# Unused bytes in the on-chip memory of an attention-and-two-MLPs kernel, so that the MLPs' operands begin at multiples of 512 bytes

## The chip, the core and the metric

The kernel runs on one core of a Trainium2 chip. The metric is the device time of one execution, in microseconds (us). Of three runs of the kernel before, the median is 1062.01 us (1061.28 to 1065.92).

On the core, TensorE (PE) multiplies: a LDWEIGHTS puts a stationary block of 128 x 128 into the array, a MATMUL streams a moving operand past it, up to 512 columns wide, and the result goes to PSUM. VectorE (DVE), ScalarE (ACT) and GpSimd (POOL) do the rest; SyncE (SP) issues most of the DMAs. Both operands of a product lie in SBUF, a memory of 128 partitions. A tile takes the same byte range of every partition, so one number, its start address within a partition, says where it lies.

## The reference

```python
def _attn_ref(q, k, v, s):                 # 4 batches, 8 heads, 576 positions, head size 64
    scores = scale * np.matmul(q, k.transpose(0, 1, 3, 2))
    cum = np.cumsum(np.maximum(s, 0.0), axis=-1)
    bias = -(cum[:, :, :, None] - cum[:, :, None, :])
    scores = np.where(causal, -1000000000.0, scores + np.minimum(bias, 0.0))
    attn = softmax(scores)
    return np.matmul(attn, v)

x = attention output as 2304 x 512
x = (relu(x @ w1_in) ** 2) @ w1_out        # 512 -> 2048 -> 512
h = x @ w2_in
return np.maximum(0.01 * h, h) @ w2_out    # 512 -> 2048 -> 512
```

All of it is float32.

## The kernel before

**Products.** Every MLP operand is split into a high and a low part in the type float32r, and a product is made of three passes (high by high, high by low, low by high: `PASSES`, L67). A weight tile is `[128, 2, 512]`: 2048 bytes of high part and 2048 bytes of low part. A stationary block is 128 columns of it, 512 bytes, so the four blocks of one part begin 512 bytes apart. A moving operand is a row of 512 columns (2048 bytes), or of 256 columns in the last of the five blocks of tokens (`BLOCKS`, L68).

**Stages.** Attention runs over 16 pairs of heads in a pipeline that is written out by hand (`attention`, L484). Its queue of matmuls is filled up with the first product of the first MLP (`up1`, L456; matmuls at L476, tile `xs` moving against `w` stationary), whose results go to DRAM as `gscr`. After the last pair the rest of that product runs. Then `down1` (L645; matmuls at L656) multiplies `gh`, which is `gscr` read back and split, moving, by the weights `wo` of `w1_out`, stationary. Then `layer2` (L666) does both products of the second MLP: at L691 `xs` moves against `w`, at L681 the activations `g` are stationary and the weights of `w2_out` move: 14 of its 16 slices lie in tiles `wo`, two in tiles `wx` (`EX = 2`, L61).

**Where the tiles lie.** The tiles are laid out in pools, one behind the other from the low end, in the order in which the pools are opened and the tiles are first asked for. First come the constants (pool `c`: `ident`, `mask`, `mask4`), then the 16 tiles `w0` to `w15` (`wpool`), then the pools of the stages. Attention's pool `at` lies above those of `up1`. The pools `s2` (staging of weights) and `w2` (the tiles `wo0` to `wo15`) are laid from the upper end downwards (`side="right"`). A tile begins at a multiple of 32 bytes. Since the constants have lengths that are no multiple of 512, and every tile of the MLPs is 2048 or 4096 bytes long, all tiles from one end share one remainder modulo 512.

In attention, each slot makes one tile `t` of scores and one small tile `m` of row minima (`maxima`, L303, `TB = 3` buffers of each), and each pair has one tile of row sums, `sums` (L329).

Of the kernel before, what the change touches and what calls it, by code (L numbers as in the profile page):

```python
# [7 lines left out]
F32 = mybir.dt.float32  # L8
# [14 lines left out]
def attention_then_two_mlps(  # L23
# [28 lines left out]
    P = 128  # L52
# [10 lines left out]
    TB, VB, YB = 3, 4, 2  # L63
# [7 lines left out]
    cpool = ctx.enter_context(tc.tile_pool(name="c", bufs=1))  # L71
# [9 lines left out]
    ident = cpool.tile([P, P], F32, name="ident")  # L81
    mask = cpool.tile([P, S], BF16, name="mask")
    mask4 = cpool.tile([P, S // 2], BF16, name="mask4")
    win, wout = {}, {}

    def bank(tag):
# [91 lines left out]
    def running_sums(at):  # L178

        sp, cum = [at.tile([BH, S], F32, tag="t", name="t", bufs=TB) for _ in range(2)]  # L180
        one, neg = [at.tile([BH, S], F32, tag="yt", name="yt", bufs=2) for _ in range(2)]
        ka = at.tile([BH, 2, S], F32R, tag="pT1", name="ka", bufs=2)
        nc.sync.dma_start(sp, s.rearrange("b h t -> (b h) t"))
        nc.gpsimd.memset(one, 1.0)
        nc.gpsimd.memset(neg, -1.0)
        yield
        nc.vector.tensor_scalar(sp, sp, 0.0, 1.0 / QK_SCALE, ALU.max, ALU.mult)
        nc.vector.tensor_tensor_scan(cum, one, sp, 0.0, ALU.mult, ALU.add)
        nc.vector.tensor_copy(ka[:, 0], cum)
        nc.vector.tensor_tensor(ka[:, 1], cum, f32(ka[:, 0]), ALU.subtract)  # L190
        nc.sync.dma_start(aug[:, 0:2, 0], one.unsqueeze(1).to_broadcast([BH, 2, S]))
        nc.sync.dma_start(aug[:, 2:4, 1], neg.unsqueeze(1).to_broadcast([BH, 2, S]))
        nc.sync.dma_start(aug[:, 0:2, 1], f32(ka))
        nc.scalar.dma_start(aug[:, 2:4, 0], f32(ka))
# [14 lines left out]
    def load_qk(at, x, i=None):  # L209

        b, g = pairs[x].b, pairs[x].g
        if not i:
            raw["q"] = at.tile([P, 2, S], F32, tag="qr", name="qr")
            raw["k"] = at.tile([P, 2, S], F32, tag="kr", name="kr")
        for src, dst, queue in ((k, raw["k"], nc.scalar if i == 0 else nc.sync), (q, raw["q"], nc.sync)):
            for e in range(2):
                for db in range(2):
                    p0 = 64 * e + 32 * db
                    dd = slice(db * 32, (db + 1) * 32)
                    if i is None:  # L220
                        nc.sync.dma_start(
                            dst[p0:p0 + 32].rearrange("p h (a d) -> p (h a) d", d=32),
                            src[b, 4 * g + 2 * e:4 * g + 2 * e + 2, :, dd].rearrange("h (a t) d -> t (h a) d", t=32))
                    else:
                        issued = queue.dma_start(
                            dst[p0:p0 + 32, i].rearrange("p (a d) -> p a d", d=32),
                            src[b, 4 * g + 2 * e + i, :, dd].rearrange("(a t) d -> t a d", t=32))
                        if queue is nc.scalar:
                            raw["issued"] = issued.ins
# [73 lines left out]
    def maxima(at, x, kind, e):  # L303

        p = pairs[x]
        t = at.tile([P, S], F32, tag="t", name="t", bufs=TB)  # L310
        m = at.tile([P, 2], F32, tag="m", name="m", bufs=TB)

        def reduce(sc, msk, a, z, first, m):
            return nc.vector.tensor_tensor_reduce(t[:, a:z], sc, msk, -QK_SCALE, first, ALU.add, ALU.min, m).ins  # L314

        sc = p.sc[e]
        if kind == 0:
            tiles = ((0, P, 0), (P, 3 * P, 1))
            for a, z, c in tiles:
                done = reduce(sc[:, a:z], mask[:, S - z + a:], a, z, 3.0e38, m[:, c:c + 1])  # L320
        elif kind == 4:
            tiles = ((0, S, 0),)
            reduce(sc[:, :S // 2], mask[:, :S // 2], 0, S // 2, 3.0e38, m[:, 1:2])
            done = reduce(p.sc[1][:, :S // 2], mask4, S // 2, S, m[:, 1:2], m[:, 0:1])
        else:
            tiles = ((0, (kind + 1) * P, 0),)
            done = reduce(sc[:, :(kind + 1) * P], mask[:, S - (kind + 1) * P:], 0, (kind + 1) * P, 3.0e38, m[:, 0:1])
        if kind == 0 and e == 0:
            p.sums = at.tile([P, 10], F32, tag="sums", name="sums", bufs=3)  # L329
        T = {0: 0, 2: 2, 3: 3, 4: 4}[kind]  # L330
        p.t = t
        return t, m, tiles, p.sums, 2 * T + e, done
# [111 lines left out]
    def up1_x(mp, j, c, bufs):  # L444

        n, w = BLOCKS[j]
        xf = mp.tile([P, W], F32, tag="xf", name="xh", bufs=2)
        nc.sync.dma_start(xf[:, :w], xscr[c, :, n:n + w])
        yield
        t = mp.tile([P, 2, W], F32R, tag="xs", name="xs", bufs=bufs)  # L450
        xs[j, c] = t
        split([t[:, z, :w] for z in range(2)], xf[:, :w])
# [3 lines left out]
    def up1(mp, j, tick=None):  # L456

        n, w = BLOCKS[j]

        def close(fc, h, gs):  # L460
            r = mp.tile([P, W], F32, tag="r", name="r", bufs=2)
            nc.scalar.activation(r[:, :w], h[:, :w], AF.Relu)
            done = nc.scalar.activation(gs[:, fc % 2, :w], r[:, :w], AF.Square)
            if fc % 2:
                nc.scalar.dma_start(gscr[fc - 1:fc + 1, :, n:n + w].rearrange("f p t -> p f t"), gs[:, :, :w])
            if tick is not None:
                tick(done.ins)

        todo = None
        for fc in range(FC):  # L470
            if fc % 2 == 0:
                gs = mp.tile([P, 2, W], F32, tag="gs", name="gs", bufs=GB1)
            h = bank("h")
            for c in range(KC):
                for y, (a, z) in enumerate(PASSES):
                    nc.tensor.matmul(h[:, :w], win[0, fc][:, a, c * P:(c + 1) * P], xs[j, c][:, z, :w],  # L476
                                     start=(c == 0 and y == 0), stop=(c == KC - 1 and y == 2))
                if c == 0 and todo is not None:
                    close(*todo)
                yield  # L480
            todo = (fc, h, gs)
        close(*todo)

    def attention(at, mg, mx):  # L484
# [14 lines left out]
        sums = running_sums(at)  # L499
        next(sums)  # L500
        load_qk(at, 0, 0)
        warm = at.tile([P, 1], F32, tag="warm", name="warm")
        nc.vector.memset(warm, 0.0)
        with after(raw["issued"]):
            nc.scalar.activation(warm, warm, AF.Exp)
# [75 lines left out]
        for y in range(end + 13):  # L581
# [11 lines left out]
            if y < end:  # L593
                args = maxima(at, x, *STEPS[st])
                live[y] = args[0]
                behind = [args[-1], exponentials(*args[:-1])]
# [114 lines left out]
    with tc.tile_pool(name="mg", bufs=1) as mg, tc.tile_pool(name="mx", bufs=1) as mx:  # L711
        with tc.tile_pool(name="at", bufs=1) as at:
            attention(at, mg, mx)
        s2, w2 = [late.enter_context(tc.tile_pool(name=x, bufs=1, side="right", reuse_waits="tile"))
                  for x in ("s2", "w2")]
        weights = Conversions(s2)
        weights.add(2, [(1, 0, fc, f"o{fc}", w2) for fc in range(FC)])
        with tc.tile_pool(name="mt", bufs=1) as mt:
            for c in range(KC):
                for _ in up1_x(mt, B, c, KC):  # L720
                    pass
            for j in (B - 1, B):
                for _ in up1(mg, j, weights.tick):
                    pass
# [42 lines left out]
```

## Time and profile before

| | |
|---|---|
| median of three runs | 1062.01 us (1061.28 to 1065.92) |
| the profiled execution: time, span | 1064.36 us, 1062.6 us |
| PE busy | 1017.2 us (96%), 5312 matmuls |
| PEld (weight loads) busy | 837.3 us (79%) |
| DVE, ACT, POOL busy | 562.6, 520.2, 225.0 us |
| mean granted TensorE clock | 0.988 |
| attention with L476 beside it | 0 to about 394 us |
| rest of L476, then L656 | about 394 to 658 us |
| L691 and L681 | 658 us to the end |

The span is the time from the first to the last instruction; the time of the profiled execution holds 1.8 us more around it. [...]

### The profile page before, as it was taken

Reading aid. Unit: us, or ns where it says so; the run is one execution under the profiler, and the core shown is the slowest. Engines: PE = TensorE matmul, PEld = TensorE weight load, DVE = VectorE, ACT = ScalarE, POOL = GpSimd, SP = SyncE. Lnnn points to the kernel's source line nnn. Section 1 sums busy time; section 2 is a strip of 40 time slices with the busy share of each in tenths; the row PEclk is TensorE's granted clock in tenths of the full one; section 3 lists DMA queues with packets and bytes.
Section 4 is the critical chain, followed back from the end, with each engine's and each line's share of the span. In section 5 each row is a group of like instructions: output and inputs, shape, how many; then the busy total and the mean of one; then the engine's idle time right before and its main releaser. Section 6 shows DMA issues by size and latency. Waiting matters only on the chain.

```text
span 1062.6 us, 15075 instructions
## 1 busy us (share of the span) xinstructions
PE 1017.2 (96%) x5312; PEld 837.3 (79%) x5312; DVE 562.6 (53%) x1262; ACT 520.2 (49%) x1126; POOL 225.0 (21%) x294
## 2 busy tenths in 40 slices
PE   5878988899999999999999999999999999999998
PEld 3656777778888878888888889888888888888897
DVE  5767868874576524787865438753222322232322
ACT  3656867876687656763443334533312322322232
POOL 6445555652232002223211003210000000000000
PEclk9988999899999999999999999999999999999999
DMA  8737384674352244866765447411100200100010
GB/s 135 102 90 151 103 168 127 135 138 123 84 109 85 81 170 168 270 191 203 237 212 167 139 117 237 129 34 30 49 1 1 80 1 1 60 1 1 1 40 21
DMA packets 152476, 111.30 MB, mean 105 GB/s; under 512 B 98992, under 2 KB 121008, under 8 KB 152400
## 3 DMA queue, kind: packets, MB, share of 16 engines
q1 hardware_dynamic: 139072, 91.01, 33.0%
q10 hardware_dynamic: 13328, 19.32, 5.3%
q8 instruction: 42, 0.69, 0.3%
q14 instruction: 34, 0.28, 0.1%
HBM read 76.69 MB, written 33.62 MB: 104 GB/s over the span
## 4 chain that ended last, share of the span: by engine, by line
PE 60%; DMA 2%; DVE 1%; ACT 0%; issue 0%; ACTq 0%; SPq 0%; DVEq 0%
PE tr L681 19%; PE h L691 9%; PE S L691 9%; PE tr L656 8%; PE h L476 6%; PE h L656 4%; PE S L656 4%; DMA wst<-in_moe_w_out_dram 1%; DMA xh<-xscr 1%; DMA gl<-gscr 0%; DMA xscr<-xo 0%; ACT xs L440 0%; DVE wo L110 0%; DVE gh L441 0%; DVE wt L108 0%
## 5 line engine op out<-in xcount | busy, mean ns | idle before, releaser
L476 PE MATMUL h<-xs,w 128*128 128x512 f32 (+1 forms) x960 | 227.6, 381 | 2.2 <-DVE w L110 0.8
L476 PEld LDWEIGHTS h<-xs,w 128*128 128x128 f32 x960 | 162.1, 190 | 33.1 <-DVE xs L441 2.2
L681 PE MATMUL tr<-wo,g 128*128 128x512 f32 x756 | 186.0, 396 | 0.0
L681 PEld LDWEIGHTS tr<-wo,g 128*128 128x128 f32 x756 | 141.5, 188 | 32.6
L107 POOL TENSOR_TENSOR wt<-wt,wst 128x512 uint32<-128x512 uint32 x64 | 88.5, 1382 | 297.2 <-DVE wt L104 238.8
L697 DVE TENSOR_TENSOR r<-S,r 128x512 f32<-128x512 f32 (+1 forms) x40 | 25.5, 639 | 173.9 <-ACT r L696 173.9
L656 PE MATMUL tr<-gh,wo 128*128 128x512 f32 (+1 forms) x576 | 114.2, 358 | 0.0
L691 PE MATMUL S<-xs,w 128*128 128x512 f32 (+1 forms) x480 | 107.2, 369 | 1.0 <-ACT xs L440 1.0
L656 PEld LDWEIGHTS tr<-gh,wo 128*128 128x128 f32 x576 | 94.7, 188 | 16.9
L691 PE MATMUL h<-xs,w 128*128 128x512 f32 (+1 forms) x480 | 107.6, 369 | 0.0
L338 ACT ACTIVATE t<-t,m 128x128 f32<-128x128 f32 (+2 forms) x144 | 83.3, 580 | 36.1 <-DVE m L314 35.6
L691 PEld LDWEIGHTS S<-xs,w 128*128 128x128 f32 x480 | 84.8, 188 | 17.4 <-ACT xs L440 1.5
L691 PEld LDWEIGHTS h<-xs,w 128*128 128x128 f32 x480 | 85.0, 188 | 16.3
L696 ACT ACTIVATE r<-S 128x512 f32<-128x512 f32 (+1 forms) x40 | 22.2, 555 | 150.6 <-PE S L691 150.6
L441 DVE TENSOR_TENSOR gh<-gl,gh 128x512 fp32r<-128x512 f32 (+1 forms) x80 | 64.5, 809 | 52.8 <-ACT gh L440 52.6
L314 DVE CUSTOM_DVE_ANT_0 t<-S,mask 128x128 f32<-128x128 f32 (+2 forms) x144 | 64.8, 481 | 45.7 <-PE S L298 22.5
L440 ACT ACTIVATE gh<-gl 128x512 fp32r<-128x512 f32 (+1 forms) x80 | 46.3, 586 | 79.2 <-PE h L656 36.5
L348 PE MATMUL tr<-ident,t 128*128 128x128 f32 x384 | 70.5, 295 | 14.3 <-ACT t L338 12.9
L441 DVE TENSOR_TENSOR g<-r,g 128x512 fp32r<-128x512 f32 (+1 forms) x80 | 51.0, 644 | 38.5 <-ACT g L440 37.0
L348 PEld LDWEIGHTS tr<-ident,t 128*128 128x128 f32 x384 | 47.1, 148 | 30.2 <-ACT t L338 17.6
L102 ACT ACTIVATE wt<-wst 128x512 f32<-128x512 f32 x64 | 42.5, 664 | 57.7 <-DMA wst<-in_moe_w_in_dram 41.6
L440 ACT ACTIVATE g<-r 128x512 fp32r<-128x512 f32 (+1 forms) x80 | 46.7, 589 | 43.5 <-DVE r L697 43.5
(105 smaller groups left out, 1462.4 us busy)
## 6 DMA issues: line engine op xcount, KB each, us to landing
wst<-in_moe_w_in_dram SPq DMA_DIRECT2D x32, 512.0 KB, 4.0
gscr<-gs ACTq DMA_DIRECT2D x32, 512.0 KB, 4.4
wst<-in_moe_w_out_dram SPq DMA_DIRECT2D x32, 512.0 KB, 4.5
gl<-gscr SPq DMA_DIRECT2D x64, 256.0 KB, 3.0
xscr<-xo SPq DMA_DIRECT2D x32, 144.0 KB, 2.5
out_dram<-o SPq DMA_DIRECT2D x18, 256.0 KB, 2.4
xh<-xscr SPq DMA_DIRECT2D x16, 256.0 KB, 2.7
zscr<-ys SPq DMA_DIRECT2D x16, 256.0 KB, 3.6
```

The costliest lines, as they stand in the source:

```text
L102: nc.scalar.activation(f32(t), f32(hw), AF.Abs)
L107: nc.gpsimd.tensor_tensor(t, t, lw, ALU.add)
L314: return nc.vector.tensor_tensor_reduce(t[:, a:z], sc, msk, -QK_SCALE, first, ALU.add, ALU.min, m).ins
L338: done = nc.scalar.activation(t[:, a:z], t[:, a:z], AF.Exp, bias=m[:, c:c + 1], scale=-1.0, accum_out=sums[:, s0:s0 + 1])
L348: nc.tensor.transpose(tr[:, c * P:(c + 1) * P], t[:, c * P:(c + 1) * P], ident)
L440: a = nc.scalar.activation(out[0], x, AF.Copy)
L441: b = nc.vector.tensor_tensor(out[1], x, f32(out[0]), ALU.subtract)
L476: nc.tensor.matmul(h[:, :w], win[0, fc][:, a, c * P:(c + 1) * P], xs[j, c][:, z, :w], start=(c == 0 and y == 0), stop=(c == KC - 1 and y = ...
L656: nc.tensor.matmul(y[e][:, :w], wout[0, fc][:, a, e * P:(e + 1) * P], gh[:, z, :w], start=(fc == 0 and x == 0), stop=(fc == FC - 1 and x = ...
L681: nc.tensor.matmul(acc[i], g[:, a, i * P:(i + 1) * P], wout[1, fc][:, z], start=(fc == 0 and x == 0), stop=(fc == FC - 1 and x == 2))
L691: nc.tensor.matmul(h[:, :w], win[1, fc][:, a, c * P:(c + 1) * P], xs[c][:, z, :w], start=(c == 0 and x == 0), stop=(c == KC - 1 and x == 2))
L697: nc.vector.tensor_tensor(r[:, :w], h[:, :w], r[:, :w], ALU.max)
```

## The change

Tiles and buffers that hold nothing are added, and small tiles are made longer:

```diff
     mask4 = cpool.tile([P, S // 2], BF16, name="mask4")
+    cpool.tile([P, 48], F32, name="pad")
...
-        m = at.tile([P, 2], F32, tag="m", name="m", bufs=TB)
+        m = at.tile([P, 16], F32, tag="m", name="m", bufs=TB + 1)
...
-            p.sums = at.tile([P, 10], F32, tag="sums", name="sums", bufs=3)
+            p.sums = at.tile([P, 16], F32, tag="sums", name="sums", bufs=4)
...
-        warm = at.tile([P, 1], F32, tag="warm", name="warm")
+        warm = at.tile([P, 64], F32, tag="warm", name="warm")[:, 0:1]
...
                   for x in ("s2", "w2")]
+        s2.tile([P, 120], F32, tag="pad", name="pad")
```

What this does to the start addresses, in bytes from the start of a partition, and in brackets the remainder modulo 512, as the two built programs have them:

| tile | role in the products | before | changed |
|---|---|---|---|
| `ident` | moving, attention's transposes | 16512 (128) | 16512 (128) |
| `w0` to `w15` | stationary at L476 and L691 | 18752 (320) and on | 18944 (0) and on |
| `xs` of `up1` | moving at L476 | (320) | (0) |
| `gh`, `xs` of `layer2` | moving at L656, L691 | 102720 (320) and on | 102912 (0) and on |
| `wx0`, `wx1` | moving at L681 | 123200, 127296 (320) | 123392, 127488 (0) |
| `g` | stationary at L681 | 131392 (320) and on | 131584 (0) and on |
| `wo0` to `wo15` | stationary at L656, moving at L681 | 151520 (480) and on | 151040 (0) and on |
| `Y` of attention | both operands at L298, moving at L288 | 182880, 192096 (96) | 183296, 192512 (0) |
| `ag0`, `last0` | operands at L298, L288 | 129344, 133952 (320) | 129536, 134144 (0) |
| `t` of attention | stationary in its transposes | (320), (64), (320) | (0), (256), (0) |
| `pT0`; `pT1` | moving at L388 | (384); (64) | (0); (256) |
| `vt` | stationary at L388 | (96) | (0) |
| `wst`, `wt` of `s2` | staging, no operand of a product | (480) | (480) |

A row of `Y` or `ag` is 2304 bytes, so the second row of such a tile begins at 256 more modulo 512 than the tile.

No instruction is added, removed or moved by this: the two programs have the same instructions in the same order on all five engines, up to the numbers of buffers and the line numbers. In their waits they differ at a few places. With a fourth buffer of `m`, 12 waits of DVE for itself at L314 are gone and one appears at L599, and POOL has one more wait at L107, for PE.

## Rows read from the trace of the kernel before

**Rows 1.** The page, parts 1 and 2: TensorE's busy time, and its granted clock by slices.
```profile
PE 1017.2 (96%) x5312; PEld 837.3 (79%) x5312; DVE 562.6 (53%) x1262; ACT 520.2 (49%) x1126; POOL 225.0 (21%) x294
...
PEclk9988999899999999999999999999999999999999
```

**Rows 2.** Windows of 40 us: stretch, then busy us by engine (instructions), clock, DMA.
```profile
0.00:40.00 40.00, 25.36 (x146) 19.20 (x146) 21.83 (x64) 17.65 (x48) 20.34 (x44) 1.00 0.83 129
40.00:80.00 40.00, 31.55 (x200) 24.95 (x200) 27.44 (x87) 24.07 (x66) 19.70 (x31) 0.91 0.47 88
...
240.00:280.00 40.00, 40.00 (x227) 33.02 (x226) 16.18 (x49) 26.77 (x62) 7.96 (x15) 1.00 0.37 109
...
840.00:880.00 40.00, 40.00 (x176) 32.75 (x176) 11.71 (x18) 10.34 (x17) 0.00 (x0) 1.00 0.02 6
```

**Rows 3.** Groups by line and shape, TensorE: busy us, mean ns | idle before, releaser.
```profile
L476 PE MATMUL h<-xs,w 128*128 128x512 f32 x768 | 203.6, 406 | 2.2 <-DVE w L110 0.8 <-ACT xs L440 0.6 <-DVE xs L441 0.4
L681 PE MATMUL tr<-wo,g 128*128 128x512 f32 x756 | 186.0, 396 | 0.0
L691 PE MATMUL h<-xs,w 128*128 128x512 f32 x384 | 94.4, 390 | 0.0
L691 PE MATMUL S<-xs,w 128*128 128x512 f32 x384 | 93.8, 390 | 1.0 <-ACT xs L440 1.0
L656 PE MATMUL tr<-gh,wo 128*128 128x512 f32 x384 | 91.0, 395 | 0.0
...
L656 PE MATMUL S<-gh,wo 128*128 128x512 f32 x192 | 50.0, 395 | 0.0
L656 PE MATMUL h<-gh,wo 128*128 128x512 f32 x192 | 50.0, 395 | 0.0
...
L681 PE MATMUL tr<-wx,g 128*128 128x512 f32 x108 | 26.3, 390 | 0.0
L476 PE MATMUL h<-xs,w 128*128 128x256 f32 x192 | 24.2, 282 | 0.0
L656 PE MATMUL tr<-gh,wo 128*128 128x256 f32 x192 | 23.2, 282 | 0.0
...
L691 PE MATMUL S<-xs,w 128*128 128x256 f32 x96 | 13.4, 283 | 0.0
L691 PE MATMUL h<-xs,w 128*128 128x256 f32 x96 | 13.3, 283 | 0.0
```

**Rows 4.** Timeline of TensorE around 760 us: start us, us, what; neighbours merged.
```profile
755.96 2.88 PE L691 MATMUL S<-xs,w 128*128 128x512 f32 x12
758.68 2.88 PE L681 MATMUL tr<-wx,g 128*128 128x512 f32 x12
761.40 2.88 PE L691 MATMUL S<-xs,w 128*128 128x512 f32 x12
...
767.97 2.97 PE L681 MATMUL tr<-wo,g 128*128 128x512 f32 x12
770.78 2.90 PE L691 MATMUL S<-xs,w 128*128 128x512 f32 x12
```

**Rows 5.** Timeline of TensorE in L656, 545 to 658 us.
```profile
545.37 44.96 PE L656 MATMUL tr<-gh,wo 128*128 128x512 f32 x192
590.16 1.56 PE L656 MATMUL S<-gh,wo 128*128 128x512 f32 x6
...
634.97 23.20 PE L656 MATMUL tr<-gh,wo 128*128 128x256 f32 x192
658.00 0.86 PE L691 MATMUL S<-xs,w 128*128 128x512 f32 x3
```

**Rows 6.** Timeline of TensorE in attention, around 302 us.
```profile
301.98 0.29 PE L288 MATMUL S<-ag,last 128*128 128x288 f32 x1
302.11 0.56 PE L288 MATMUL S<-Y,last 128*128 128x288 f32 x3
302.50 0.30 PE L288 MATMUL S<-ag,last 128*128 128x288 f32 x1
```

## The prediction

> **What bounds the kernel now.** I read the page first: TensorE is busy for 96% of the span, and after the first ten slices it is granted full clock in nearly all of it [rows 1]. A busy share is only an upper bound, so the windows come next. From 240 us on PE is busy in 40.00 of 40 us, at clock 1.00, while DVE, ACT, POOL and the DMA engines fall far below that: in the window 840 to 880 us they have 11.71, 10.34 and 0.00 us and a share of 0.02 [rows 2]. Before 240 us PE has gaps (25.36 and 31.55 us of 40). The groups by shape say the same of the MLPs' products: idle time before L656 and L681 is 0.0, before L691 it is 1.0 us in all [rows 3]. So from about 394 us to the end, two thirds of the span, the time is the number of matmuls times the distance from one to the next, and nothing else can shorten it but that distance.
>
> The last step is therefore to read this distance, by the starts of neighbouring rows of the timeline. In layer 2, 12 matmuls at L691 take 758.68 - 755.96 = 2.72 us, which is **226.7 ns** each. The next 12, at L681 with the moving tile `wx`, take 761.40 - 758.68 = 2.72 us, again 226.7 ns. A little later 12 at the same line with the same stationary tile `g`, but with the moving tile `wo`, take 770.78 - 767.97 = 2.81 us, **234.2 ns** [rows 4]. Same instruction, same width, same clock, no wait between them. In the first MLP's second product 192 matmuls with `wo` as stationary tile take 590.16 - 545.37 = 44.79 us, **233.3 ns** [rows 5]. What the slow rows share is the tile `wo`. By the table of addresses, `wo` is the one MLP tile that begins at another remainder (480) than its partner (320); `wx`, which does the same work at 226.7 ns, begins at 320 like `g`. This contrast is what the prediction rests on.
>
> **The change part by part.** No instruction is added, removed or moved, so every term is a change in how long something takes.
>
> 1. *L681 with `wo`.* 756 matmuls [rows 3]. Both operands now begin at remainder 0, as both of `wx` and `g` begin at 320 today. At the distance of the `wx` rows each saves 234.2 - 226.7 = 7.5 ns: **-5.7 us**. All of it lies on the path, since PE has no idle time there.
> 2. *L656, 512 wide.* 384 + 192 + 192 = 768 matmuls [rows 3], each from 233.3 to 226.7 ns: 6.6 ns, **-5.1 us**, again with no idle time beside it.
> 3. *L656, 256 wide.* 192 matmuls take 658.00 - 634.97 = 23.03 us, 119.9 ns each, although `wo` is in them too [rows 5]. Their mean busy time per instruction is the same as in L476 and L691 at that width (282 and 283 ns, while 512-wide rows with `wo` have 395 or 396 against 390) [rows 3]. So at this width a different remainder costs nothing that shows, and I take **0**.
> 4. *L691, L476 and L681 with `wx`.* They move from 320 and 320 to 0 and 0. If the cost comes from the two operands beginning differently, nothing changes: **0**. This is the unknown price of the change, and the trace bounds it only from afar. From below, the part of a matmul that doesn't grow with its width: 226.7 ns at 512 columns and 119.9 at 256 give 0.417 ns per column and 13.1 ns on top, so at best 13.1 ns of each could go. From above, the 7.5 ns by which the dearest rows seen lie over theirs. I take 0 because the nearest row, equal remainders, is that of these very matmuls.
> 5. *Attention's own products.* Their rows begin at other remainders than their partners, too: at L288 those of `Y` at 352 or 480 and those of `ag` at 64 or 192, against 320 of `last`. Three matmuls of `Y` take 302.50 - 302.11 = 0.39 us, 130 ns each; the one of `ag` before them takes 302.11 - 301.98 = 0.13 us [rows 6]. The line through the two widths of term 4 gives 13.1 + 288 x 0.417 = 133 ns for 288 columns. These rows stand on that line and not above it, so there is nothing to be won: **0**.
> 6. *L476 inside attention.* Here a 512-wide matmul may overlap the weight load of an attention product from `Y` or `vt`, whose remainder differs from its own; after the change it does not. Bounds: nothing, and 7.5 ns for each of the 768 at L476, which is 5.8 us. Most of them follow another of L476, and before 240 us PE has gaps that would swallow a gain. I take **-1 us**.
> 7. *Waits, staging, transfers.* Twelve waits of DVE for itself go and one comes; what such a wait costs isn't in the rows. DVE has 27.44 us of work in 40 where attention is tightest [rows 2]; PE after 240 us is full and doesn't wait for it. One more wait on POOL stands at L107, where POOL is idle for most of its time (7.96 us of 40 at 240 us, none at 840) and weights are made far ahead. Transfers now begin at rounder addresses; their share is 0.02 to 0.83 and only in the first 40 us are they near a limit [rows 2]. **0**, with 1 us to either side.
>
> Sum: -5.7 - 5.1 - 1 = **-11.8 us**. The profiled execution took 1064.36 us, so it would take 1052.6. It stands 2.35 us above the median of the three runs; against that median of 1062.01 the sum gives **1050.2 us**.
>
> [...] The rows show that with nothing but the place of the moving tile changed, 12 matmuls take 2.81 us in place of 2.72 [rows 4]. [...]
>
> **The rivals.**
>
> *A. No change (1061 to 1062 us).* The slow rows share `wo`, but the address isn't the only thing that sets `wo` apart: it lies in the upper part of the memory, above 151520, and `wx` lies below 130000. If the distance in memory and not the remainder makes 234.2 of 226.7, the padding doesn't help, for the tiles stay in their regions. For it: one row of `wx` against one of `wo` can't tell the two apart. Against it: the extra is much the same whichever of the 14 or 16 tiles is used, since a run of 192 matmuls over all `wo` has one mean, 233.3 [rows 5]; a cost of distance should not be so even, nor vanish at 256 columns. In this case too the change doesn't do what it says.
>
> *B. More than forecast (1000 to 1045 us).* If a start at a full multiple of 512 also takes away what equal starts at 320 leave, all 3744 matmuls of the MLPs (768 + 768 + 768 + 864 of 512 columns and 576 of 256 [rows 3]) lose up to 13.1 ns. That is 49 us more than the sum, 1001 us; half of it gives 1026. For it: the operands at 320 straddle a multiple of 512 in every block of 128 columns, and at 0 none does. Against it: 13.1 ns at both widths looks like a fixed price of changing weights.
>
> *C. Slower (1074 us).* Equal starts at 0 may make both reads of PE meet at the same place of the memory with every block, where 320 did not. The price is that of the slow rows: the 768 + 768 + 108 matmuls of 512 columns that now run at 226.7 ns go to 234.2, +12.3 us, and the ones with `wo` stay. It decides if a meeting depends on the address and not on the difference of two addresses. Against it: `xs` with `w` and `wx` with `g` share their remainder today and are the fastest rows there are.
>
> **How the numbers follow.** The forecast has 0.62, A 0.15, B 0.13 and C 0.10. The forecast's own range is 1046 to 1056: the 5.8 us of term 6 as its far end, 1 us for term 7, and, since attention has stretches at half clock (0.91 in the window from 40 us [rows 2], some 7 us at half, worth up to 3.5 us) that may fall otherwise. The range for 8 in 10 runs from 1034, into the part of B where less than half of it comes true, to 1065, A with the spread of the runs shown; C and the far half of B stay outside. A measurement of this kernel can tell about 0.5% from no change, 5.3 us. Faster by more than that: the forecast without a small tail, and B, 0.75. Within it: A and the tail, 0.16. Slower: C without its tail, 0.09.
>
> **What would show it.** In the changed kernel's timeline, 12 matmuls at L681 (one line lower there) with `wo` should take 2.72 us from start to start, like those with `wx`, and 192 at L656 43.5 us in place of 44.79; L691 should stay at 2.72. Mean busy times in the groups of 512 columns should all read 390. If `wo` still takes 2.81, A is true and the theory of the remainder is wrong. If L691 falls below 2.72, it is B; if it rises, C. The prediction is also wrong if the matmuls speed up and the end doesn't come earlier: then idle time before L656 or L681 must have appeared, most likely on ACT's or DVE's splits.

## The result, and the profile after

The changed kernel takes **1046.09 us** (median of five runs, 1044.2 to 1048.92), the kernel before, in five runs, 1062.96 us (1061.28 to 1065.92). The ratio is 0.9845, with a 95% interval of 0.9826 to 0.9865: 1.55% faster, 16.5 us. Forecast were 1050.2 us and a gain of 11.8 us. The profiled execution took 1046.09 us, its span is 1044.3 us, its mean granted clock 0.992 (0.988 before). In a second set of five runs the changed kernel had the ratio 0.9835 (0.9809 to 0.9862).

The page after, parts 1 and 2, answers to [rows 1]:

```profile
PE 1002.3 (96%) x5312; PEld 834.2 (80%) x5312; DVE 558.3 (53%) x1262; ACT 519.5 (50%) x1126; POOL 226.1 (22%) x294
...
PEclk9999999899999999999999999999999999999999
```

PE's busy time fell by 14.9 us, the span by 18.3. The other engines have the work that they had. Where it went is seen in the groups by shape; their lines stand one lower than in [rows 3]:

```profile
L477 PE MATMUL h<-xs,w 128*128 128x512 f32 x768 | 203.9, 406 | 2.9 <-DVE w L111 1.3 <-ACT xs L441 1.0 <-ACT r L463 0.2
L682 PE MATMUL tr<-wo,g 128*128 128x512 f32 x756 | 180.9, 389 | 0.0
L692 PE MATMUL h<-xs,w 128*128 128x512 f32 x384 | 94.0, 389 | 0.0
...
L657 PE MATMUL tr<-gh,wo 128*128 128x512 f32 x384 | 88.7, 390 | 0.0
...
L657 PE MATMUL S<-gh,wo 128*128 128x512 f32 x192 | 49.1, 390 | 0.4 <-DVE gh L442 0.4
L657 PE MATMUL h<-gh,wo 128*128 128x512 f32 x192 | 48.7, 389 | 0.0
...
L682 PE MATMUL tr<-wx,g 128*128 128x512 f32 x108 | 26.3, 389 | 0.0
...
L657 PE MATMUL tr<-gh,wo 128*128 128x256 f32 x192 | 23.2, 283 | 0.0
```

The groups with `wo`, which had means of 395 and 396 ns, now have 389 and 390, like the rest. `xs` with `w` (L477) has its 406 as before, so term 6 of the prediction, a gain of this product inside attention, is not seen there.

The timeline of TensorE in layer 2, which answers to [rows 4], and in the first MLP's second product, to [rows 5] (start us, us, what). A single 512-wide row lasts 389 or 390 ns here and the next begins about 227 ns after it, so the rows overlap, and times are taken from start to start:

```profile
744.68 2.88 PE L682 MATMUL tr<-wx,g 128*128 128x512 f32 x12
747.40 2.88 PE L692 MATMUL S<-xs,w 128*128 128x512 f32 x12
...
753.98 2.88 PE L682 MATMUL tr<-wo,g 128*128 128x512 f32 x12
756.70 2.88 PE L692 MATMUL S<-xs,w 128*128 128x512 f32 x12
```

```profile
535.23 43.68 PE L657 MATMUL tr<-gh,wo 128*128 128x512 f32 x192
578.75 1.52 PE L657 MATMUL S<-gh,wo 128*128 128x512 f32 x6
```

Twelve with `wx` take 747.40 - 744.68 = 2.72 us, twelve with `wo` 756.70 - 753.98 = 2.72 us, and the 192 at L657 take 43.52 us, 226.7 ns each. That is what the prediction asked for.

The stages are divided by the first matmul of L656 and the first of L691, one line lower in the changed kernel. The first row here is of before (its L691 begins at 658.00 us [rows 5]), the others of the changed kernel:

```profile
437.18 3.19 PE L656 MATMUL tr<-gh,wo 128*128 128x512 f32 x13
```

```profile
428.46 3.82 PE L657 MATMUL tr<-gh,wo 128*128 128x512 f32 x16
...
645.30 0.86 PE L692 MATMUL S<-xs,w 128*128 128x512 f32 x3
```

Between the two profiled executions, attention with the product beside it lost 8.7 us, the rest of that product with L656 lost 4.0, layer 2 lost 5.6. Forecast were 1, 5.1 and 5.7. The MLPs did about what was said. The 8.7 us are one pair of executions, and attention scatters: in the first kernel below, whose attention has the tiles of before, L656 begins at 433.48 us and not at 437.18. The ratio of all runs gives 16.5 us, so that beside the 9.6 us of the MLPs some 7 are left for attention. That is still far more than said, and the experiments have two questions: does the MLPs' gain come from equal starts or from the multiple of 512, and what did attention gain from?

### The profile page after: what moved, and what is told of

Read it like the earlier page. It is cut to its first block, busy times and chain, and to the rows that moved or that the text cites. A ratio compares the mean times of both kernels' runs of the same rounds, so it can differ in the third digit from the quotient of the medians.

```text
span 1044.3 us, 15068 instructions
## 1 busy us (share of the span) xinstructions
PE 1002.3 (96%) x5312; PEld 834.2 (80%) x5312; DVE 558.3 (53%) x1262; ACT 519.5 (50%) x1126; POOL 226.1 (22%) x294
## 4 chain that ended last, share of the span: by engine, by line
PE 56%; DMA 4%; DVE 2%; issue 1%; ACT 1%; POOL 0%; ACTq 0%; SPq 0%; DVEq 0%; POOLq 0%
PE tr L682 19%; PE h L692 9%; PE S L692 9%; PE h L477 6%; PE tr L657 6%; PE S L657 3%; PE h L657 3%; DMA wst<-in_moe_w_in_dram 2%; DMA wst<-in_moe_w_out_dram 1%; DVE wt L109 1%; DMA gl<-gscr 1%; ACT wt L103 0%; DMA xh<-xscr 0%; DVE gh L442 0%; DMA xscr<-xo 0%
## 5 line engine op out<-in xcount | busy, mean ns | idle before, releaser
L477 PE MATMUL h<-xs,w 128*128 128x512 f32 (+1 forms) x960 | 228.0, 382 | 2.9 <-DVE w L111 1.3
L477 PEld LDWEIGHTS h<-xs,w 128*128 128x128 f32 x960 | 162.7, 191 | 33.0 <-DVE w L111 2.1
L682 PE MATMUL tr<-wo,g 128*128 128x512 f32 x756 | 180.9, 389 | 0.0
L682 PEld LDWEIGHTS tr<-wo,g 128*128 128x128 f32 x756 | 141.1, 188 | 28.8
L657 PE MATMUL tr<-gh,wo 128*128 128x512 f32 (+1 forms) x576 | 111.9, 354 | 0.0
L692 PE MATMUL S<-xs,w 128*128 128x512 f32 (+1 forms) x480 | 106.9, 368 | 1.1 <-ACT xs L441 1.1
L692 PE MATMUL h<-xs,w 128*128 128x512 f32 (+1 forms) x480 | 107.3, 368 | 0.0
L657 PEld LDWEIGHTS tr<-gh,wo 128*128 128x128 f32 x576 | 94.8, 189 | 14.6
L692 PEld LDWEIGHTS S<-xs,w 128*128 128x128 f32 x480 | 84.8, 188 | 16.9 <-ACT xs L441 1.6
L692 PEld LDWEIGHTS h<-xs,w 128*128 128x128 f32 x480 | 84.9, 188 | 15.7
L442 DVE TENSOR_TENSOR gh<-gl,gh 128x512 fp32r<-128x512 f32 (+1 forms) x80 | 62.2, 780 | 48.0 <-ACT gh L441 47.5
```

The lines of the kernel that those rows point to most:

```text
L442: b = nc.vector.tensor_tensor(out[1], x, f32(out[0]), ALU.subtract)
L657: nc.tensor.matmul(y[e][:, :w], wout[0, fc][:, a, e * P:(e + 1) * P], gh[:, z, :w], start=(fc == 0 and x == 0), stop=(fc == FC - 1 and x = ...
L682: nc.tensor.matmul(acc[i], g[:, a, i * P:(i + 1) * P], wout[1, fc][:, z], start=(fc == 0 and x == 0), stop=(fc == FC - 1 and x == 2))
L692: nc.tensor.matmul(h[:, :w], win[1, fc][:, a, c * P:(c + 1) * P], xs[c][:, z, :w], start=(c == 0 and x == 0), stop=(c == KC - 1 and x == 2))
```

## The experiments

### Equal starts or multiples of 512

In the first kernel `wo` gets the remainder of its partners, which is no multiple of 512, and nothing else moves. It is the kernel before with one line more:

```diff
                   for x in ("s2", "w2")]
+        s2.tile([P, 40], F32, tag="pad", name="pad")
```

> The kernel before with 160 unused bytes in s2 and nothing else, so that wo begins at 320 like its partners; no operand begins at a multiple of 512. Difference theory (a 512-wide product is slow where its two operands begin at different remainders): L656 and L681 at 226.7 ns a matmul, attention untouched, some 10 us less than before, ratio about 0.991. Multiples theory (an operand must begin at a multiple of 512): 233 to 234 ns as before, ratio 1.00.

Measured: 1053.05 us, ratio 0.9892 (0.9862 to 0.9923). The timeline of this kernel in layer 2:

```profile
755.91 2.88 PE L681 MATMUL tr<-wx,g 128*128 128x512 f32 x12
758.63 2.88 PE L681 MATMUL tr<-wo,g 128*128 128x512 f32 x12
761.36 2.88 PE L691 MATMUL S<-xs,w 128*128 128x512 f32 x12
```

`wo` takes 2.73 us, `wx` 2.72: 160 unused bytes are enough for the whole gain of the MLPs. From the first matmul of L656 to the end this execution takes 1049.0 - 433.48 = 615.5 us, the changed kernel 1044.3 - 428.46 = 615.8, and before it was 1062.6 - 437.18 = 625.4. The second kernel moves the partners to `wo` instead:

```diff
     mask4 = cpool.tile([P, S // 2], BF16, name="mask4")
+    cpool.tile([P, 40], F32, name="pad")
```

> The kernel before with 160 unused bytes behind the constants: every MLP operand begins at 480, which is no multiple of 64. Difference theory: 226.7 ns at L476, L656, L691 and L681 alike, so 10 us of gain in the MLPs. Multiples theory: 233 ns or more everywhere, also at L691 that had 226.7: 12 us or more lost there. Attention's tiles move too (qr and kr begin 224 past a multiple of 256), so the stage up to the first matmul of L656 is read apart from the rest.

Measured: 1056.55 us, ratio 0.9923 (0.9895 to 0.9951). The timeline:

```profile
762.72 2.88 PE L682 MATMUL tr<-wx,g 128*128 128x512 f32 x12
765.44 2.88 PE L682 MATMUL tr<-wo,g 128*128 128x512 f32 x12
768.16 2.88 PE L692 MATMUL S<-xs,w 128*128 128x512 f32 x12
```

All have 2.72 us, with every operand at 480, and from the first matmul of L657 to the end it takes 1055.8 - 440.66 = 615.1 us, like the first kernel. So the operands need not begin at a multiple of 512: with both at 320 and with both at 480 twelve take the 2.72 or 2.73 us that they take with both at 0. The third kernel is the changed one without its line in `s2`:

```diff
-        s2.tile([P, 120], F32, tag="pad", name="pad")
```

> The changed kernel without the unused bytes in s2: wo back at 480, all else at 0. Difference theory: L657 and L682 (lines of this file) back at 233 to 234 ns, some 10 us slower than the changed kernel, 1055 to 1057 us; attention keeps its gain of some 9 us. Were the two gains one thing, attention's would go too.

Measured: 1058.36 us, ratio to before 0.9941 (0.9922 to 0.996). Twelve with `wo` are back at 2.80 us (762.46 to 765.26):

```profile
759.74 2.88 PE L682 MATMUL tr<-wx,g 128*128 128x512 f32 x12
762.46 2.96 PE L682 MATMUL tr<-wo,g 128*128 128x512 f32 x12
765.26 2.91 PE L692 MATMUL S<-xs,w 128*128 128x512 f32 x12
```

By the ratios it is 10 to 11 us slower than the changed kernel (by the medians of the two sets 12, and a little over the 1055 to 1057 us that were expected), and 0.6%, some 6 us, faster than before, which is attention's part; 9 were expected of it. The two gains are separate things: 1 - 0.9892 from `wo` alone and 1 - 0.9941 without it add to 0.0167, against 0.0155 and 0.0165 for the whole change in its two sets.

### How alike must the starts be

The fourth kernel asks this in one run: each of the tiles `wo` begins 32 bytes further than its neighbour, modulo 512.

```diff
+        if which == 1 and str(slot)[0] == "o" and slot != "o0" and f"gap{slot}" not in gaps:
+            gaps[f"gap{slot}"] = pool.tile([P, 8], F32, tag=f"gap{slot}", name=f"gap{slot}")
         t = pool.tile([P, 2, DM], F32R, tag=f"w{slot}", name=f"w{slot}")
```

> The changed kernel with 32 unused bytes more between neighbouring tiles wo, so that wo0 begins at 32, wo1 at 64 and so on to wo14 at 480 and wo15 at 0, while gh and g stay at 0. Difference theory: L659 and L684 (lines of this file) run at 226.7 ns with wo15 and slower with the others, by the remainder of each; whether a difference of 64, 128 or 256 bytes costs too is open and read from the starts of each twelve. Theory of one granule: all multiples of 64 (wo1, wo3, ...) at 226.7, all odd multiples of 32 (wo0, wo2, ...) at 231 or more.

A single execution, 1056.28 us. The timeline of one block of layer 2; `g` begins at 0, and the rows with `wo` are, in this order, `wo0` (at 32), `wo1` (64), `wo6` (224) and `wo7` (256):

```profile
757.48 2.88 PE L684 MATMUL tr<-wx,g 128*128 128x512 f32 x12
760.20 2.97 PE L684 MATMUL tr<-wo,g 128*128 128x512 f32 x12
763.00 2.92 PE L694 MATMUL S<-xs,w 128*128 128x512 f32 x12
765.76 2.93 PE L684 MATMUL tr<-wo,g 128*128 128x512 f32 x12
768.52 1.79 PE L694 MATMUL h<-xs,w 128*128 128x512 f32 x7
...
792.31 2.96 PE L684 MATMUL tr<-wo,g 128*128 128x512 f32 x12
795.11 2.91 PE L694 MATMUL h<-xs,w 128*128 128x512 f32 x12
797.86 2.88 PE L684 MATMUL tr<-wo,g 128*128 128x512 f32 x12
800.58 2.88 PE L694 MATMUL S<-xs,w 128*128 128x512 f32 x12
```

From start to start, twelve take 2.72 us with `wx` (difference 0), 2.80 at 32, 2.76 at 64, 2.80 at 224 and again **2.72 at 256**. The granule that I had put beside the difference theory, 64 bytes, is wrong: 64 costs 2.76, and 128 (`wo3`) costs 2.79 (775.71 to 778.50 us). What has to agree is the start **modulo 256**. In this scan no difference but 0 and 256 was free for 512-wide products: by the starts of all rows with `wo` in layer 2, a matmul takes 227 ns at 256 and 230 to 234 at the other remainders from 32 to 448 (230 or 231 at 64 and at 320). The 256-wide products of L659 take 115 to 120 ns whatever the remainder.

The row behind a slow one is slow as well, although its own operands agree: 765.76 - 763.00 = 2.76 us with `xs` and `w`, and 797.86 - 795.11 = 2.75. By the single starts in the trace this is a matter of its first matmuls: of the twelve from 763.00 us on, seven have 224 to 241 ns and the last five 226 or 227. Why it carries over stays open.

The single starts also tell which stationary block counts. In layer 2 of the kernel before and of the changed one the next weight load starts 2 to 4 ns after a matmul does and its row lasts 188 ns, so the block of the following matmul is loaded within the 227 ns up to that matmul's start. At L659 the last matmul with `wo7` (256, which agrees with `gh` at 0) is followed by one with `wo8` (288): it takes 235 ns, behind others of 226 and 227. The last with `wo14` (480) is followed by one with `wo15` (0): it takes 227 ns, behind others of 231 to 234. At both places the time goes by whether the moving operand agrees with the block that is loaded beside it, that of the next matmul.

### What attention gained from

The landing times of the loads tell the changed kernel from the one before (issues by tile: what, count, KB each, median us from issue to landing). Before:

```profile
kr<-in_k_dram SPq DMA_DIRECT2D x28, 144.0 KB, 4.0
qr<-in_q_dram SPq DMA_DIRECT2D x28, 144.0 KB, 5.4
```

After:

```profile
kr<-in_k_dram SPq DMA_DIRECT2D x28, 144.0 KB, 2.9
qr<-in_q_dram SPq DMA_DIRECT2D x28, 144.0 KB, 4.5
```

`load_qk` (L209) writes q and k in runs of 32 floats, 128 bytes. The tiles `qr` and `kr` began at 173632 and 178240, 64 bytes past a multiple of 256, so every run lay across a multiple of 128 and every other run across a multiple of 256 (the table of addresses above leaves these two tiles out). They now begin at 173824 and 178432, which are multiples of 256, and no run lies across either. In the trace the 73728 DMA packets of 128 bytes, which are these loads, take 17.3 ns on average before and 13.0 in the changed kernel; those of 11 to 13 ns are 62% of them before and 99% in the changed kernel. So the packets' times and the landing times go with the start of the two tiles. Why, and whether the multiple of 128 or that of 256 counts, is not shown: in the runs the tiles begin at a multiple of 256 (`kr` lands after 2.9 to 3.3 us), or 64 or 224 bytes past one (4.0 to 4.3 us).

The fifth kernel takes this away again, in the changed kernel, and leaves all else:

```diff
+            if x == 0:
+                at.tile([P, 16], F32, tag="gap", name="gap")
             raw["q"] = at.tile([P, 2, S], F32, tag="qr", name="qr")
...
-        warm = at.tile([P, 64], F32, tag="warm", name="warm")[:, 0:1]
+        warm = at.tile([P, 48], F32, tag="warm", name="warm")[:, 0:1]
```

> The changed kernel with the raw tiles qr and kr of attention alone moved by 64 bytes, so that they again begin 64 past a multiple of 256 and half of their 128-byte runs cross one. Transfer theory (attention gained because the loads of q and k land earlier): landing of kr and qr back from 2.9 and 4.5 to 4.0 and 5.4 us, and most of attention's 8.7 us lost, 1052 to 1055 us. Theory of buffers (m and sums have one more) or of attention's own products: the time of the changed kernel, 1046 us.

Measured: 1051.86 us, ratio 0.9888 (0.9853 to 0.9922), some 5 to 6 us slower than the changed kernel (1046.09 and 1046.61 in its two sets) and at the fast end of the 1052 to 1055 expected. Its packets of 128 bytes take 17.0 ns on average. Its loads:

```profile
kr<-in_k_dram SPq DMA_DIRECT2D x28, 144.0 KB, 4.0
qr<-in_q_dram SPq DMA_DIRECT2D x28, 144.0 KB, 5.5
```

The sixth does the reverse: the kernel before, with those two tiles alone at multiples of 256.

```diff
+            if x == 0:
+                at.tile([P, 48], F32, tag="gap", name="gap")
             raw["q"] = at.tile([P, 2, S], F32, tag="qr", name="qr")
...
-        warm = at.tile([P, 1], F32, tag="warm", name="warm")
+        warm = at.tile([P, 88], F32, tag="warm", name="warm")[:, 0:1]
```

> The kernel before with 192 unused bytes ahead of qr and 320 in the tile warm behind kr: the two raw tiles of attention begin at a multiple of 256, every other tile of attention keeps its remainder, and wo stays at 480. Transfer theory: kr and qr land after 3 and 4.5 to 4.9 us, and 4 to 6 us less than before in all, ratio 0.994 to 0.996. Theory of buffers or of attention's own products: no change.

Measured: 1058.22 us, ratio 0.9951 (0.9933 to 0.9969), 4.5 us less than the 1062.72 of before beside it. Its packets of 128 bytes take 12.9 ns on average.

```profile
kr<-in_k_dram SPq DMA_DIRECT2D x28, 144.0 KB, 2.9
qr<-in_q_dram SPq DMA_DIRECT2D x28, 144.0 KB, 4.2
```

Both ways round, the start of `qr` and `kr` is worth 4.5 to 6 us. What a load that lands a microsecond sooner brings forward is seen in part in the queue that issues it. SyncE's rows in the kernel before, for one set of eight loads and what stands behind them:

```profile
47.25 2.57 SPq L221 DMA_DIRECT2D kr<-in_k_dram  x4
49.92 5.39 SPq L221 DMA_DIRECT2D qr<-in_q_dram  x4
55.42 0.73 SPq L118 DMA_DIRECT2D wst<-in_moe_w_in_dram  x1
```

In the changed kernel:

```profile
44.73 2.62 SPq L222 DMA_DIRECT2D kr<-in_k_dram  x4
47.45 3.15 SPq L222 DMA_DIRECT2D qr<-in_q_dram  x4
50.71 1.77 SPq L119 DMA_DIRECT2D wst<-in_moe_w_in_dram  x1
```

And in the fifth kernel, with the two tiles 64 bytes off:

```profile
46.59 2.60 SPq L224 DMA_DIRECT2D kr<-in_k_dram  x4
49.30 5.37 SPq L224 DMA_DIRECT2D qr<-in_q_dram  x4
54.77 0.70 SPq L119 DMA_DIRECT2D wst<-in_moe_w_in_dram  x1
```

Behind the four loads of k, SyncE needs 5.39 us to issue the four of q before, 5.37 in the fifth kernel and 3.15 in the changed one, and what stands behind them on this queue comes that much sooner after the first load. Of the seven such sets this is the one with the largest difference: all 28 issues of q together take 34.7 us before, 34.2 in the fifth kernel, 28.3 in the changed one and 30.4 in the sixth, so the average set gains about 1 us. The first 60 us of the four kernels (before, changed, `qr` and `kr` 64 off, those two alone at 256) have the DMA engines busy by these shares, the last column but one:

```profile
0.00:60.00 60.00, 42.30 (x260) 32.65 (x260) 35.39 (x108) 29.13 (x78) 29.00 (x58) 1.00 0.81 125
```

```profile
0.00:60.00 60.00, 42.44 (x282) 32.88 (x282) 38.60 (x117) 32.87 (x87) 31.10 (x61) 1.00 0.67 135
```

```profile
0.00:60.00 60.00, 43.53 (x260) 33.25 (x260) 35.55 (x109) 30.00 (x80) 29.04 (x58) 0.97 0.79 125
```

```profile
0.00:60.00 60.00, 43.66 (x280) 33.67 (x282) 38.33 (x117) 32.66 (x86) 30.75 (x61) 0.97 0.66 129
```

With the aligned tiles the share is 0.66 or 0.67 and PE has done 280 or 282 matmuls by then; without, 0.79 or 0.81 and 260. Over the first 240 us the share is 0.56 or 0.57 with the aligned tiles and 0.63 without, while the granted clock is 0.95 or 0.96 in all four, so the clock doesn't make the difference. Which wait carries it forward from there is not shown. None of the longer waits in these 240 us follows the two tiles alone: ACT's waits for staged weights, for one, sum to 20.0 us before, but to 14.6, 14.8 and 14.5 in the three others.

The seventh kernel tries the other thing that the change did to attention, the additional buffers, in the kernel before; 416 unused bytes between the two keep every other remainder:

```diff
-        m = at.tile([P, 2], F32, tag="m", name="m", bufs=TB)
+        m = at.tile([P, 2], F32, tag="m", name="m", bufs=TB + 1)
...
+        if kind == 0 and e == 0 and x == 0:
+            at.tile([P, 104], F32, tag="gap", name="gap")
...
-            p.sums = at.tile([P, 10], F32, tag="sums", name="sums", bufs=3)
+            p.sums = at.tile([P, 10], F32, tag="sums", name="sums", bufs=4)
```

> The kernel before with one buffer more of m and of sums, and unused bytes behind them so that all other tiles keep their remainders. Transfer theory: no change, ratio 0.998 to 1.002. Theory of buffers: attention gains 4 to 9 us, ratio 0.992 to 0.996.

Measured: ratio 1.0003 (0.9987 to 1.002), 1063.31 us. The 12 waits of DVE for itself cost nothing that shows.

### What is left, and whether more is to be had

Four kernels ran beside each other in one set. First the changed kernel again:

> The changed kernel itself, beside the three others of this set: 0.983 to 0.987 of before.

Measured: 1046.61 us, 0.9835 (0.9809 to 0.9862). Beside it the kernel before with the two starts alone that the runs point to, which are the additions of the first and the sixth kernel together:

> The kernel before with the two starts alone that the runs so far point to: wo at 320 like its partners (160 unused bytes in s2), and qr and kr at a multiple of 256; every other tile of attention and of the MLPs keeps its remainder. If these two are all of the change, the ratio is that of the changed kernel beside it, to 0.002. If attention gains from its other tiles too, it is up to 0.004 slower.

Measured: 1048.7 us, 0.9856 (0.983 to 0.9882). That is 0.0021 from the changed kernel, a little over the mark that I had set and well inside both intervals: by the ratios the two starts make 87% of the change (0.0144 of 0.0165), and whether the remaining 2 us are real can't be told from these runs. Then the changed kernel with attention's products and v's loads 32 bytes off again:

```diff
-        warm = at.tile([P, 64], F32, tag="warm", name="warm")[:, 0:1]
+        warm = at.tile([P, 8], F32, tag="warm", name="warm")[:, 0:1]
```

> The changed kernel with the tile warm short again, so that Y, vt, pT0, pX, xo and vr of attention begin 32 past a multiple of 256 while qr and kr stay at one and the MLPs are untouched. If attention's products or v's loads gain from a start at 0: 2 to 4 us slower than the changed kernel. If q and k are all: no change, within 0.002 of its ratio.

Measured: 1048.85 us, 0.9841 (0.9814 to 0.9869). By the ratio no change; by the medians 2 us, which these intervals don't resolve either.

Two kernels try for more. One, of an earlier set, has the staging tiles of the weights at 0, too:

```diff
         s2, w2 = [late.enter_context(tc.tile_pool(name=x, bufs=1, side="right", reuse_waits="tile"))
...
-        s2.tile([P, 120], F32, tag="pad", name="pad")
...
             for j in (B - 1, B):
                 for _ in up1(mg, j, weights.tick):
                     pass
+        s2.tile([P, 120], F32, tag="pad", name="pad")
```

> The changed kernel with the unused bytes of s2 at the other end of that pool, so that the staging tiles wst and wt of s2 begin at 0 too and wo stays at 0. If the conversions of the weights wait for their loads on the path anywhere, a gain of up to 2 us; I expect none, the time of the changed kernel (1046 us, ratio 0.983 to 0.987), since PE has no idle time where these tiles are used.

Measured: 1047.12 us, 0.9847 (0.9823 to 0.987), no change. The other, the fourth of the set, has the identity of the transposes at 0:

```diff
+    cpool.tile([P, 96], F32, name="pad0")
     ident = cpool.tile([P, P], F32, name="ident")
...
-    cpool.tile([P, 48], F32, name="pad")
+    cpool.tile([P, 80], F32, name="pad")
```

> The changed kernel with unused bytes ahead of ident too, so that the identity of attention's transposes begins at 0 like the tiles t (0 and 256) that it is multiplied with; all other remainders stay but those of the masks. If an equal remainder modulo 256 helps a product of 128 columns: the 384 transposes of L350 (line of this file) follow each other faster than 109 ns and up to 2 us go. I expect nothing, since 256-wide products show no difference.

Measured: 1049.27 us, 0.9852 (0.983 to 0.9874), no gain; the transposes follow each other after 109 ns (median) here as in the changed kernel and in the one before. No version was found that beats the changed kernel.

## Why the prediction was right, and what it missed

The time lies in the stated range and on the forecast side. By the mechanism, terms 1 and 2 were right; that the time lies just inside the forecast's own range (1046 to 1056 us) is luck, for its lower end was made for term 6, the clock (0.50 from 62 to 68 us in the kernel before) and 1 us of term 7, and what filled it was the 4.5 to 6 us of term 7.

- *Terms 1 and 2* (L681 and L656 with `wo`: -5.7 and -5.1 us) held. Twelve at L682 went from 2.81 to 2.72 us, and layer 2 lost 5.6 us between the two profiled executions, by the starts 5.0 in the rows with `wo` and 0.5 in those of L691. L657 went from 233.3 to 226.7 ns; its stage lost 4.0 us and not 5.1, for new idle time before L657, 0.4 us by the page, took some of it back. This was the one visible sign of "what is late next": PE once waits for DVE's split of `gh`.
- *Term 3* (nothing at 256 columns) held: that group has a mean of 282 ns before and 283 after.
- *Term 4* (nothing for operands that agreed already) held but for the 0.5 us at L691, whose rows no longer follow slow ones, and with it rivals B and C fell: L692 is still at 2.72 us, and the kernels with all operands at 320 or at 480 have the same distance as the one with all at 0.
- *Rival A* fell with the first kernel: `wo` stayed in its region, only its remainder changed.
- *Term 7 is the step that failed in size.* It gave transfers 0, with 1 us to either side, on the ground that their share was near a limit in the first 40 us alone. It measured 4.5 to 6 us. The row was read rightly, 0.83, but a share below a limit doesn't show that a faster transfer brings nothing: over the first 240 us it was 0.63 and fell to 0.57. No term read the price of a transfer from its packets or its landing. The lengths of the runs stood in the code, and where they begin in the built program.
- *Term 6* (-1 us from L476 in attention) is not seen: its group has 406 ns before and after.
- *A row read too widely:* from 240 us on PE is not busy in 40.00 of 40 us everywhere; the windows 360 to 400 and 640 to 680 us have 38.90 and 38.95. No term rests on it.

Of the 16.5 us measured, then, some 10 come from the MLPs as worked out, nothing that shows from term 6, and 4.5 to 6 from term 7, which had 0 in the sum; what is left can't be told from the scatter of the runs.

## What to carry to other kernels

Where TensorE is busy without a gap, compare the distance from start to start of matmuls of one shape with different operands: a few nanoseconds between them, here 7 of 234, are worth a per cent of the time and may cost some unused bytes to remove. What to make equal is the start of the moving tile and of the stationary one that is loaded beside it, modulo 256 bytes; here both at 320 or both at 480 did as well as both at 0 (2.72 or 2.73 us for twelve). Runs here show it for float32r products of 512 columns alone. For tiles that a DMA fills in short runs, look where the runs begin: here, with runs of 128 bytes, tiles at a multiple of 256 bytes in place of 64 past one were worth 4.5 to 6 us.

## What the runs showed of the hardware that was not expected

- For float32r products of 512 columns whose weight loads run beside them, a difference of the two starts (moving operand, and stationary block loaded meanwhile) that is no multiple of 256 bytes costs 3 to 8 ns of each matmul over 226.7; 256 itself costs nothing (2.72 us for twelve at a difference of 0 and of 256, 2.76 at 64, 2.80 at 32 and 224). Products of 256 columns show none of it (119.9 ns with a difference of 160 bytes, 115 to 120 at every multiple of 32).
- The cost also falls on the first matmuls behind a slow row, whose own operands agree: the twelve there take 2.75 and 2.76 us in place of 2.72.
- Moving two DMA targets by 64 bytes changed the landing of 144 KB in runs of 128 bytes from 2.9 to 4.0 us (`kr`), the mean time of a packet of 128 bytes from 13.0 to 17.0 ns, and the median time in which SyncE issues one load of q from 0.75 to 0.98 us.
